# Talking-heads attention with a gated layer: row transfers four partitions higher, loads from SyncE, fp16 pairs in all mixes, rows five units ahead

## The chip, the cores and the metric

The kernel runs on one core of a Trainium2 chip. The metric is the device time of one execution in microseconds. The core's engines are TensorE (PE, with its weight loads shown apart as PEld), VectorE (DVE), ScalarE (ACT), GpSimd (POOL) and SyncE (SP, which only issues DMAs here). Each engine works through its own instructions in order; an instruction that waits holds up all that stand behind it on its engine. PSUM (the banks that TensorE writes to) has eight banks.

## The reference

Four batches, twelve heads, 448 positions, 64 elements per head. The scores of all heads are mixed with each other before the softmax (`w_pre`) and the probabilities after it (`w_post`); the result goes through a gated layer of 1792 tokens, 768 to 1536 to 768.

```python
scores = scale * np.matmul(q, k.transpose(0, 1, 3, 2))
scores = np.einsum('bhij,hg->bgij', scores, w_pre)
scores = scores - np.max(scores, axis=-1, keepdims=True)
attn = np.exp(scores)
attn = attn / (np.sum(attn, axis=-1, keepdims=True) + 1e-09)
attn = np.einsum('bhij,hg->bgij', attn, w_post)
x = np.matmul(attn, v)                       # then (B*S, H*D)
gate = 1.0 / (1.0 + np.exp(-(x @ w_gate)))
out = (gate * (x @ w_val)) @ w_out
```

The weights of the gated layer come as 64-bit floats and are converted on the core.

## The kernel before

**Blocks and units.** Each batch's 448 query rows are cut into blocks of 120, 120, 120 and 88 rows, 16 blocks in all. A block is cut into *units* of two row sets of ten rows each; a batch has 23 units (6 + 6 + 6 + 5; the last holds one set), the kernel 92.

**What is done to a block and a unit.** `scores` multiplies q and k of two heads (six such jobs per block, L149), and `keep` copies them to an SBUF buffer `st`, one head by ACT and one by DVE (L155). There are two `st` buffers, for even and odd blocks. To mix heads on TensorE, the heads of a row must lie across partitions: `regroup` (L179 to L185) does this with DMAs from `st` to a tile `T`, one per half x: 120 partitions for a unit of two sets (five rows of twelve heads each, twice), and, for such a unit, two more DMAs of four partitions (7 KB each) that complete T's second part to 124 partitions. `premix` (L194) multiplies T by the first mix, into one PSUM bank `pm` per set; `rowmax` (L199, DVE) takes the negative maximum; `expo` (L206, ACT) the exponential with its row sum; `norm` (L211 POOL, L212 DVE) one over that sum. `scale` then multiplies by it on POOL, in one of two ways. For units 6 to 83 (`pairs`) it writes an fp16 high half `ph` of the scaled probabilities (L222), `p_lo` (L234, DVE) the fp16 low half `pl`, and `postmix` (L246) is three fp16 products per set, key block and half. For the first 6 and the last 8 units it scales the small second mix matrix instead (`w2s`, L227), and `postmix` is one float32 product with the exponentials themselves. `mix` (L254, ACT) copies the result from the pair of banks `mx` to SBUF. There is one such pair, so the next unit's `postmix` waits for this copy. `av` (L269) multiplies a finished block by v, 16 matmuls per job, and ACT scales the result (L277) and stores it as x in device memory (L278).

**What sets the order.** The loop over slots s issues, in this order: the rows of unit s + LEAD (LEAD = 4; three T buffers); `norm` and `scale` of unit s + 1; `premix` and `rowmax` of unit s + 2; a score job of the next block and its two copies between the exponentials of unit s + 2; `p_lo` of unit s + 1; the loads that are planned for this slot; the gated layer's work that is due; `postmix` of unit s; `mix` of unit s; `av`, and with it the scaling and the store of x. The loads are planned at L291 to L302: v at a batch's slots 4, 6 and 8, k of the next batch in six slots, q four slots ahead of its block's scores.

**Queues.** The rows go from SP's queue. q, k, v, x and the first four raw weight tiles of the gated layer go from ACT's, and so in ACT's own order: each load stands there between the exponentials and the `mix` copy of its slot. The gated layer's x tiles of the first two batches are read back from POOL's queue (L821).

**The gated layer** (`_Moe`) is planned by list scheduling before anything is issued (`order_tasks`). Its matrices are kept as sums of two rounded parts (ACT rounds, L824; DVE takes the rest, L827) and multiplied in seven products per block instead of eight. Raw weights are loaded (L787), converted by ACT and DVE (L795 to L806), written out once and read back. `ROOM` gives the number of buffers of each kind that come free at four times; V is one of the kinds for weight parts. The first of this work runs beside the last units of the attention.

Of the kernel before, what the change touches and what calls it, by code (L numbers as in the profile page):

```python
# [22 lines left out]
R = 10  # L23
# [18 lines left out]
def _attention(ctx, tc, ins, B, H, S, D, xs, raws, make_moe):  # L42
# [18 lines left out]
                          for n, b in (("t", 3), ("e", 3), ("p", 2), ("s", 4)))  # L61
# [64 lines left out]
    def k_load(b, c, eng=None):  # L126
        t = kst.tile([128, S], F32, tag="k", name="k")
        (eng or nc.scalar).dma_start(out=t, in_=kp[b, c])
        k_t[b, c] = t

    def q_load(bi, eng=None):

        b, i0, _, _, sets = blocks[bi]
        n = R * sets
        t = qst.tile([128, NP * QB], F32, tag="q", name="q")
        (eng or nc.scalar).dma_start(out=t[:, :NP * n], in_=qp[b, :, NP * i0:NP * (i0 + n)])
        q_t[bi] = t[:, :NP * n].rearrange("p (c s) -> p c s", s=n)
# [22 lines left out]
    def v_load(b, u):  # L160
        t = vst.tile([128, QUAD, 4, D], F32, tag="v", name="v")
        nc.scalar.dma_start(out=t.rearrange("p h j d -> p (h j d)"), in_=vb[b, u])
# [3 lines left out]
    t_t, nm_t, e_t, ss_t, p_t, mx_t = {}, {}, {}, {}, {}, {}  # L166
    mixes = [mp.tile([128, 4, H, QB], F32, name=f"mix{i}") for i in range(2)]

    def pairs(u):

        return PB + 2 <= u < NU - 8

    def regroup(u):
        bi, r0s, _, _, i = units[u]
        sets, st = blocks[bi][4], st_t[bi]
        T = tp.tile([128, 2, S], F32, tag="T", name="T")
        for x in range(2):
            if len(r0s) == 2:
                nc.sync.dma_start(out=T[:2 * HK, x], in_=st[i + x:sets * R:sets])  # L179
            else:  # L180
                nc.sync.dma_start(out=T[:HK, x], in_=st[i + sets * HALF * x:sets * HALF * (x + 1):sets])
        if len(r0s) == 2:
            p = i + sets * HALF
            for x in range(2):
                nc.sync.dma_start(out=T[2 * HK:64 + HK, x], in_=st[p + x:p + x + 1, :64 - HK])  # L185
        t_t[u] = T

    def premix(u):
        T = t_t.pop(u)
        banks = units[u][2]  # L190
        for x in range(2):
            for i, bank in enumerate(banks):
                rows = slice(64 * i, 64 * i + HK)
# [20 lines left out]
    def scale(u):  # L214

        p_t[u] = []
        for i in range(len(units[u][1])):
            e, ss = e_t[u][:, i], ss_t[u][:, i:i + 1]
            if pairs(u):
                if i == 0:  # L220
                    ph = pp.tile([128, 2, S], F16, tag="ph", name="ph")
                nc.gpsimd.tensor_scalar(ph[:, i], e, ss, 1.0, op0=ALU.mult, op1=ALU.mult)  # L222
                p_t[u].append(ph[:, i])
            else:
                if i == 0:
                    w = pp.tile([128, 2, HK], F32, tag="ph", name="w2s")
                nc.gpsimd.tensor_scalar(w[:, i], w2, ss, 1.0, op0=ALU.mult, op1=ALU.mult)  # L227
                p_t[u].append((e, w[:, i]))

    def p_lo(u):  # L230
        if pairs(u):
            pl = pp.tile([128, 2, S], F16, tag="pl", name="pl")
            for i, ph in enumerate(p_t[u]):
                nc.vector.scalar_tensor_tensor(pl[:, i], e_t[u][:, i], ss_t[u][:, i:i + 1], ph,  # L234
                                               op0=ALU.mult, op1=ALU.subtract)
                p_t[u][i] = (ph, pl[:, i])

    def postmix(u):
        mx = two_banks(ps_mx, "mx").rearrange("p x (i c) -> p x i c", i=2)[:, :, :, :4 * HK]
        for i, (a, b) in enumerate(p_t.pop(u)):  # L240
            terms = [(a, w2hi), (a, w2lo), (b, w2hi)] if pairs(u) else [(a, b)]
            for jb in range(4):
                for k, (lhs, w) in enumerate(terms):
                    for x in range(2):
                        rows = slice(64 * x, 64 * x + 64)
                        nc.tensor.matmul(mx[:, x, i, jb * HK:(jb + 1) * HK], lhsT=lhs[rows, JB[jb]:JB[jb] + 128], rhs=w[rows],  # L246
                                         start=(k == 0), stop=(k == len(terms) - 1))
# [12 lines left out]
    def av(bi, c):  # L260
# [10 lines left out]
        if c % 4 == 3 or c == KC - 1:  # L271
# [6 lines left out]
            nc.scalar.dma_start(out=xs[b, c0:c + 1, :, i0:i0 + n].rearrange("c p s -> p c s"), in_=xt)  # L278


    LEAD = 4
# [51 lines left out]
    q_load(1)  # L333
# [643 lines left out]
```

## Time and profile before

| | |
|---|---|
| median of 3 runs | 876.36 us (872.37 to 903.53) |
| profiled execution | 877.92 us, span 876.1 us, mean granted TensorE clock 0.971 |
| PE busy | 830.4 us, 95% |
| DVE busy | 658.4 us, 75% |
| ACT busy | 557.8 us, 64% |
| POOL busy | 138.5 us, 16% |
| DMA | 136.74 MB, mean 156 GB/s |

The span is the time from the first to the last instruction on the core. A busy PE is not PE at its peak. The granted clock is a share of 2.4 GHz; its lower level is half, 1.2 GHz. Shares are means over stages with different limits: attention to about 396 us, then the gated layer. Where a row ends in square brackets, it tells how long the engine sat idle before that instruction and what released it; releasers are inferred from semaphore events.

### The profile page before, as it was taken

Reading aid. Unit: us, or ns where it says so; the run is one execution under the profiler, and the core shown is the slowest. Engines: PE = TensorE matmul, PEld = TensorE weight load, DVE = VectorE, ACT = ScalarE, POOL = GpSimd, SP = SyncE. Lnnn points to the kernel's source line nnn. Section 1 sums busy time; section 2 is a strip of 40 time slices with the busy share of each in tenths; the row PEclk is TensorE's granted clock in tenths of the full one; section 3 lists DMA queues with packets and bytes.
Section 4 is the critical chain, followed back from the end, with each engine's and each line's share of the span. In section 5 each row is a group of like instructions: output and inputs, shape, how many; then the busy total and the mean of one; then the engine's idle time right before and its main releaser. Section 6 shows DMA issues by size and latency. Waiting matters only on the chain.

```text
span 876.1 us, 22591 instructions
## 1 busy us (share of the span) xinstructions
PE 830.4 (95%) x9314; PEld 647.7 (74%) x9314; DVE 658.4 (75%) x1003; ACT 557.8 (64%) x967; POOL 138.5 (16%) x284
## 2 busy tenths in 40 slices
PE   8989988999899978899999999959999999999998
PEld 2555555565556545689899999949999999999997
DVE  4487887888788866259888788999786676579970
ACT  3678786888788777566776679845544444454640
POOL 0143443434344435210000000000000000000000
PEclk9999999999999999669999999979999999999999
DMA  5375457545754565721655668875251222200001
GB/s 169 143 238 184 158 168 240 183 160 180 248 169 162 185 233 198 268 71 39 241 210 181 208 216 288 296 272 202 82 182 55 66 64 63 73 19 1 32 31 64
DMA packets 70335, 136.74 MB, mean 156 GB/s; under 512 B 19000, under 2 KB 50648, under 8 KB 70232
## 3 DMA queue, kind: packets, MB, share of 16 engines
q1 hardware_dynamic: 49176, 108.17, 35.4%
q10 hardware_dynamic: 20288, 24.37, 9.2%
q0 software_dynamic: 768, 2.75, 1.1%
q8 instruction: 73, 1.20, 0.6%
q14 instruction: 30, 0.25, 0.1%
HBM read 70.14 MB, written 25.17 MB: 109 GB/s over the span
## 4 chain that ended last, share of the span: by engine, by line
PE 80%; DMA 7%; ACT 5%; DVE 4%; SPq 2%; issue 1%; ACTq 1%; DVEq 0%
PE bank L837 35%; PE bank L848 15%; PE mx L246 8%; PE av L269 8%; PE pm L194 8%; PE qk L149 5%; DMA T<-st 5%; ACT mix L254 2%; DMA raws<-in_w_dram 2%; SPq L179 1%; ACT e L206 1%; DVE m_GV L827 1%; DVE m_FWTR L830 1%; DMA k<-in_kp_dram 1%; ACT st L155 1%
## 5 line engine op out<-in xcount | busy, mean ns | idle before, releaser
L837 PE MATMUL bank<-m_GV 128*128 128x448 f32 x1512 | 310.6, 367 | 1.3 <-DVE m_GV L827 0.7
L837 PEld LDWEIGHTS bank<-m_GV 128*128 128x128 f32 x1512 | 284.1, 188 | 27.3 <-DVE m_GV L827 1.1
L827 DVE TENSOR_TENSOR m_GV<-m_FWTR,m_GV 128x768 fp32r<-128x768 f32 (+1 forms) x139 | 156.0, 1135 | 53.6 <-ACT m_GV L824 53.3
L824 ACT CAST m_GV<-m_FWTR 128x768 fp32r<-128x768 f32 (+1 forms) x139 | 134.3, 980 | 62.3 <-DVE m_FWTR L830 24.2
L848 PE MATMUL bank<-m_GV 128*128 128x448 f32 x756 | 161.0, 375 | 9.3 <-ACT m_GV L824 8.2
L848 PEld LDWEIGHTS bank<-m_GV 128*128 128x128 f32 x756 | 145.4, 193 | 24.6 <-ACT m_GV L824 8.9
L206 ACT ACTIVATE e<-pm,nm 128x448 f32<-128x448 f32 x180 | 114.8, 638 | 59.1 <-DVE nm L199 50.5
L199 DVE TENSOR_REDUCE nm<-pm 128x1 f32<-128x448 f32 x180 | 104.0, 619 | 52.3 <-PE pm L194 50.8
L254 ACT ACTIVATE mix<-mx 128x960 f32<-128x960 f32 (+1 forms) x92 | 102.6, 1116 | 31.7 <-PE qk L149 9.6
L246 PEld LDWEIGHTS <-ph 64*128 64x128 f16 x2448 | 56.3, 93 | 72.7 <-issue 40.2
L854 ACT COPY m_FWTR<-bank 128x448 f32<-128x448 f32 x96 | 51.2, 533 | 80.7 <-PE bank L837 57.7
L222 POOL TENSOR_SCALAR ph<-e,ss 128x448 f16<-128x448 f32 x153 | 96.2, 642 | 33.1 <-DVE ss L212 24.0
L194 PE MATMUL pm<-T,w 60*64 60x448 f32 x720 | 96.9, 576 | 1.9 <-DMA T<-st 1.8
L269 PE MATMUL av<-mix,v 128*64 128x120 f32 (+1 forms) x1504 | 97.3, 276 | 0.0
L234 DVE SCALAR_TENSOR_TENSOR pl<-e,ss,ph 128x448 f16<-128x448 f32 x153 | 97.3, 676 | 0.0
L149 PE MATMUL qk<-k,q 64*64 64x448 f32 (+2 forms) x640 | 94.0, 548 | 2.5 <-ACT st L155 2.1
L269 PEld LDWEIGHTS av<-mix,v 128*64 128x64 f32 x1504 | 77.6, 143 | 6.8 <-issue 2.4
L857 DVE TENSOR_TENSOR m_FWTR<-bank,m_FWTR 128x448 f32<-128x448 f32 x90 | 55.9, 622 | 35.5 <-PE bank L848 21.0
L246 PE MATMUL mx<-w2hi,ph 64*128 64x60 f16 x1224 | 60.1, 188 | 20.8 <-ACT mix L254 20.7
L830 DVE TENSOR_TENSOR m_FWTR<-m_FWTR 128x768 f32<-128x768 f32 (+1 forms) x67 | 77.4, 1167 | 0.1
L149 PEld LDWEIGHTS qk<-k,q 64*64 64x64 f32 (+2 forms) x640 | 27.1, 135 | 50.2 <-issue 30.0
L246 PE MATMUL mx<-w2hi,pl 64*128 64x60 f16 x1224 | 59.7, 187 | 0.0
(58 smaller groups left out, 687.0 us busy)
## 6 DMA issues: line engine op xcount, KB each, us to landing
T<-st SPq DMA_DIRECT2D x176, 210.0 KB
raws<-in_w_dram SPq DMA_DIRECT2D x32, 767.6 KB
w<-m_FWTR SPq DMA_DIRECT2D x36, 384.0 KB
m_FWTR<-w SPq DMA_DIRECT2D x30, 384.0 KB
raws<-w SPq DMA_DIRECT2D x18, 384.0 KB
v<-in_vb_dram ACTq DMA_DIRECT2D x12, 512.0 KB
out_dram<-m_FWTR SPq DMA_DIRECT2D x24, 224.0 KB
k<-in_kp_dram ACTq DMA_DIRECT2D x18, 224.0 KB
```

The source lines that it names most:

```text
L149: nc.tensor.matmul(sc[e][s0:s1, :S], lhsT=q[rows, c, s0:s1], rhs=k[rows, :], start=True, stop=True)
L194: nc.tensor.matmul(pm[bank][64 * x:64 * x + 64, :S], lhsT=w1[rows], rhs=T[rows, x], start=True, stop=True)
L199: nc.vector.tensor_reduce(nm[:, i:i + 1], pm[bank][:, :S], axis=AX.X, op=ALU.max, negate=True)
L206: nc.scalar.activation(out=e_t[u][:, i], in_=pm[units[u][2][i]][:, :S], func=AF.Exp, bias=nm_t[u][:, i:i + 1], scale=1.0, accum_out=ss_t[u ...
L234: nc.vector.scalar_tensor_tensor(pl[:, i], e_t[u][:, i], ss_t[u][:, i:i + 1], ph, op0=ALU.mult, op1=ALU.subtract)
L246: nc.tensor.matmul(mx[:, x, i, jb * HK:(jb + 1) * HK], lhsT=lhs[rows, JB[jb]:JB[jb] + 128], rhs=w[rows], start=(k == 0), stop=(k == len(te ...
L254: nc.scalar.activation(out=out.rearrange("p g (y r) -> p y g r", r=HALF), in_=mx_t.pop(u), func=AF.Copy, scale=1.0 / (P_UP * W_UP))
L269: nc.tensor.matmul(av_t[bi][64 * i:64 * i + 64, c % 4, :n], lhsT=vt[b, u][:, h + i, jb, :], rhs=mixes[bi % 2][:, jb, 2 * c + i, :n], start ...
L824: self.nc.scalar.copy(self.f32(hi).bitcast(F32R), self.f32(f))
L827: self.nc.vector.tensor_tensor(self.f32(lo).bitcast(F32R), self.f32(f), self.f32(hi), op=ALU.subtract)
L837: self.nc.tensor.matmul(self.f32(bank), lhsT=w[a][:, k], rhs=x[b][:, k], start=self.START[i] and k == r == 0, stop=k == self.KH - 1 and r ...
L848: self.nc.tensor.matmul(self.f32(bank), lhsT=w[a][:, k], rhs=b[bb], start=self.START[i] and j == k == r == 0, stop=j == OUT_TILES - 1 and ...
```

## The change

It makes seven edits. T's rows lie at partitions 4 to 123 instead of 0 to 119: the first set at 4 to 63, the second at 64 to 123. The first mix's matmul for the first set now reads partitions 0 to 63, of which the first four are zero in T (set once by POOL) and in the matrix, so the two four-partition transfers fall away. There are four T buffers, used in turn. Every unit uses fp16 pairs. All loads and the stores of x are issued by SP, but for the three small mix matrices and the second block's q tile, which stay with ACT. LEAD is 5. In `ROOM`, V has one buffer less from 15 slots before the layer and one more at its start. Beside this the names move: `t_t` and `pairs` are gone.

```diff
-                          for n, b in (("t", 3), ("e", 3), ("p", 2), ("s", 4)))
+                          for n, b in (("t", 1), ("e", 3), ("p", 2), ("s", 4)))
...
     def k_load(b, c, eng=None):
...
-        (eng or nc.scalar).dma_start(out=t, in_=kp[b, c])
+        (eng or nc.sync).dma_start(out=t, in_=kp[b, c])
...
     def q_load(bi, eng=None):
...
-        (eng or nc.scalar).dma_start(out=t[:, :NP * n], in_=qp[b, :, NP * i0:NP * (i0 + n)])
+        (eng or nc.sync).dma_start(out=t[:, :NP * n], in_=qp[b, :, NP * i0:NP * (i0 + n)])
...
     def v_load(b, u):
...
-        nc.scalar.dma_start(out=t.rearrange("p h j d -> p (h j d)"), in_=vb[b, u])
+        nc.sync.dma_start(out=t.rearrange("p h j d -> p (h j d)"), in_=vb[b, u])
...
-    t_t, nm_t, e_t, ss_t, p_t, mx_t = {}, {}, {}, {}, {}, {}
+    nm_t, e_t, ss_t, p_t, mx_t = {}, {}, {}, {}, {}
...
-    def pairs(u):
-        return PB + 2 <= u < NU - 8
+    t_bufs = [tp.tile([128, 2, S], F32, name=f"T{i}") for i in range(4)]
+    for T in t_bufs:
+        nc.gpsimd.memset(T[:64 - HK], 0.0)
     def regroup(u):
...
-        sets, st = blocks[bi][4], st_t[bi]
-        T = tp.tile([128, 2, S], F32, tag="T", name="T")
+        sets, st, T = blocks[bi][4], st_t[bi], t_bufs[u % len(t_bufs)]
+        at = 64 - HK
...
-                nc.sync.dma_start(out=T[:2 * HK, x], in_=st[i + x:sets * R:sets])
+                nc.sync.dma_start(out=T[at:at + 2 * HK, x], in_=st[i + x:sets * R:sets])
...
-                nc.sync.dma_start(out=T[:HK, x], in_=st[i + sets * HALF * x:sets * HALF * (x + 1):sets])
-        if len(r0s) == 2:
-            p = i + sets * HALF
-            for x in range(2):
-                nc.sync.dma_start(out=T[2 * HK:64 + HK, x], in_=st[p + x:p + x + 1, :64 - HK])
-        t_t[u] = T
+                nc.sync.dma_start(out=T[at:at + HK, x], in_=st[i + sets * HALF * x:sets * HALF * (x + 1):sets])
     def premix(u):
-        T = t_t.pop(u)
+        T = t_bufs[u % len(t_bufs)]
...
-                rows = slice(64 * i, 64 * i + HK)
+                rows = slice(64, 64 + HK) if i else slice(0, 64)
...
     def scale(u):
-        p_t[u] = []
+        ph = pp.tile([128, 2, S], F16, tag="ph", name="ph")
...
-            e, ss = e_t[u][:, i], ss_t[u][:, i:i + 1]
-            if pairs(u):
-                if i == 0:
-                    ph = pp.tile([128, 2, S], F16, tag="ph", name="ph")
-                nc.gpsimd.tensor_scalar(ph[:, i], e, ss, 1.0, op0=ALU.mult, op1=ALU.mult)
-                p_t[u].append(ph[:, i])
-            else:
-                if i == 0:
-                    w = pp.tile([128, 2, HK], F32, tag="ph", name="w2s")
-                nc.gpsimd.tensor_scalar(w[:, i], w2, ss, 1.0, op0=ALU.mult, op1=ALU.mult)
-                p_t[u].append((e, w[:, i]))
+            nc.gpsimd.tensor_scalar(ph[:, i], e_t[u][:, i], ss_t[u][:, i:i + 1], 1.0, op0=ALU.mult, op1=ALU.mult)
+        p_t[u] = [ph]
     def p_lo(u):
-        if pairs(u):
-            pl = pp.tile([128, 2, S], F16, tag="pl", name="pl")
-            for i, ph in enumerate(p_t[u]):
-                nc.vector.scalar_tensor_tensor(pl[:, i], e_t[u][:, i], ss_t[u][:, i:i + 1], ph,
-                                               op0=ALU.mult, op1=ALU.subtract)
-                p_t[u][i] = (ph, pl[:, i])
+        pl = pp.tile([128, 2, S], F16, tag="pl", name="pl")
+        for i in range(len(units[u][1])):
+            nc.vector.scalar_tensor_tensor(pl[:, i], e_t[u][:, i], ss_t[u][:, i:i + 1], p_t[u][0][:, i],
+                                           op0=ALU.mult, op1=ALU.subtract)
+        p_t[u].append(pl)
     def postmix(u):
         mx = two_banks(ps_mx, "mx").rearrange("p x (i c) -> p x i c", i=2)[:, :, :, :4 * HK]
-        for i, (a, b) in enumerate(p_t.pop(u)):
-            terms = [(a, w2hi), (a, w2lo), (b, w2hi)] if pairs(u) else [(a, b)]
+        ph, pl = p_t.pop(u)
+        for i in range(len(units[u][1])):
...
-                for k, (lhs, w) in enumerate(terms):
+                for k, (p, w) in enumerate(((ph, w2hi), (ph, w2lo), (pl, w2hi))):
...
-                        nc.tensor.matmul(mx[:, x, i, jb * HK:(jb + 1) * HK], lhsT=lhs[rows, JB[jb]:JB[jb] + 128], rhs=w[rows],
-                                         start=(k == 0), stop=(k == len(terms) - 1))
+                        nc.tensor.matmul(mx[:, x, i, jb * HK:(jb + 1) * HK], lhsT=p[rows, i, JB[jb]:JB[jb] + 128], rhs=w[rows],
+                                         start=(k == 0), stop=(k == 2))
...
-            nc.scalar.dma_start(out=xs[b, c0:c + 1, :, i0:i0 + n].rearrange("c p s -> p c s"), in_=xt)
-    LEAD = 4
+            nc.sync.dma_start(out=xs[b, c0:c + 1, :, i0:i0 + n].rearrange("c p s -> p c s"), in_=xt)
+    LEAD = 5
...
-    q_load(1)
+    q_load(1, nc.scalar)
...
-    ROOM = ((-15, dict(F=5, G=4, W=6, V=4)), (-7, dict(G=2, V=2, T=3)), (0, dict(G=3, W=2, V=2)), (9.6, dict(F=4, G=5, W=2, V=0, T=4, R=0)))
+    ROOM = ((-15, dict(F=5, G=4, W=6, V=3)), (-7, dict(G=2, V=2, T=3)), (0, dict(G=3, W=2, V=3)), (9.6, dict(F=4, G=5, W=2, V=0, T=4, R=0)))
...
     def load_raw(self, k):
-        self.loads.dma_start(out=self.at["raw", k].bitcast(I8)[:, :8 * self.WE - 3], in_=self.src[k].bitcast(I8)[:, 3:])
+        self.nc.sync.dma_start(out=self.at["raw", k].bitcast(I8)[:, :8 * self.WE - 3], in_=self.src[k].bitcast(I8)[:, 3:])
     def top(self, k, step):
...
-            (self.nc.gpsimd if p == 0 else self.nc.sync).dma_start(out=out[:, :, e], in_=src.rearrange("c p s -> p c s"))
+            self.nc.sync.dma_start(out=out[:, :, e], in_=src.rearrange("c p s -> p c s"))
...
     def slot(self, t):
...
-        self.loads = self.nc.scalar if a < -7 else self.nc.sync
...
-            w1[(60 * x + r * H + np.arange(H) - 64) % 60 + 64 if x else at, r * H:(r + 1) * H] = w_pre
+            w1[at.start + 4 * (1 - x):at.stop + 4 * (1 - x), r * H:(r + 1) * H] = w_pre
...

```

**Order on ACT, slots 6 and 7 of the first batch.** The names are the exponential (L206, e), the score copy (L155, st), the loads and the copy of the mix (L254). The brackets hold what an instruction waits for; DMAHW0 to DMAHW7 are semaphores that DMAs of both queues share in turn. Before:

```order
L206 ACTIVATE e,ss<-pm_114,nm 128x448 [waits DVE_49]
L162 DMA v<-in_vb_dram 128x1024 [waits DMAHW6_49]
L128 DMA k<-in_kp_dram 128x448 [waits DMAHW7_49]
L254 ACTIVATE mix_125<-mx 128x4x48x5 [waits PE_49]
L206 ACTIVATE e,ss<-pm_112,nm 128x448 [waits DVE_49,Activation_49,Pool_49]
L155 COPY st<-qk 120x448 [waits PE_49]
L206 ACTIVATE e,ss<-pm_113,nm 128x448 [waits DVE_49]
L128 DMA k<-in_kp_dram 128x448 [waits DMAHW1_49]
L254 ACTIVATE mix_125<-mx 128x4x48x5 [waits PE_49]
```

Now, in the same place (the first copy of a new block waits for the row transfers that read this buffer):

```order
L201 ACTIVATE e,ss<-pm_114,nm 128x448 [waits DVE_49]
L239 ACTIVATE mix_125<-mx 128x4x48x5 [waits PE_49]
L201 ACTIVATE e,ss<-pm_112,nm 128x448 [waits DVE_49,Activation_49,Pool_49]
L155 COPY st<-qk 90x448 [waits DMAHW4_49,DMAHW3_49,DMAHW5_49,DMAHW2_49,DMAHW6_49,DMAHW1_49,DMAHW7_49,DMAHW0_49,PE_49]
L201 ACTIVATE e,ss<-pm_113,nm 128x448 [waits DVE_49]
L239 ACTIVATE mix_125<-mx 128x4x48x5 [waits PE_49]
```

The loads between the exponentials and the mix copy are gone from ACT.

**Order on SP, in the second batch, around the last unit of a block.** A number after st tells the block whose buffer is read, one after T the buffer. Before:

```order
L185 DMA T_2594<-st_1820 4x1x448 x2
L179 DMA T_2687<-st_1820 120x1x448 x2
L185 DMA T_2687<-st_1820 4x1x448 x2
L179 DMA T_2782<-st_1820 120x1x448 x2
L185 DMA T_2782<-st_1820 4x1x448 x2
L179 DMA T_2874<-st_2341 120x1x448 x2
```

Now:

```order
L179 DMA T3_129<-st_1882 120x1x448 x2
L136 DMA q_2575<-in_qp_dram 128x540
L263 DMA xs_60<-xt_2635 128x4x88
L179 DMA T0_126<-st_1882 120x1x448 x2
L162 DMA v_2667<-in_vb_dram 128x1024
L179 DMA T1_127<-st_1882 120x1x448 x2
L128 DMA k_2757<-in_kp_dram 128x448
L263 DMA xs_60<-xt_2817 128x2x88
L179 DMA T2_128<-st_1882 120x1x448 x2
L162 DMA v_2849<-in_vb_dram 128x1024
L128 DMA k_2851<-in_kp_dram 128x448
L179 DMA T3_129<-st_2394 120x1x448 x2
```

The four-partition transfers are gone, and loads and stores of x stand between the rows; the block's last rows (T2_128) come right behind a store of x.

**Order on DVE, two of the last units.** Named are the maxima (nm), one over the sum (ss), the converted raw weights (m_FWTR<-raws) and the low halves (pl). Before:

```order
L212 RECIPROCAL ss<-ss 128x2
L199 TENSOR_REDUCE nm<-pm_114 128x1
L199 TENSOR_REDUCE nm<-pm_112 128x1
L212 RECIPROCAL ss<-ss 128x2
L199 TENSOR_REDUCE nm<-pm_113 128x1
L199 TENSOR_REDUCE nm<-pm_114 128x1
L806 SCALAR_TENSOR_TENSOR m_FWTR<-raws 128x768 x2
```

Now:

```order
L219 SCALAR_TENSOR_TENSOR pl<-e,ss,ph 128x448 x2
L791 SCALAR_TENSOR_TENSOR m_FWTR<-raws 128x768 x2
L207 RECIPROCAL ss<-ss 128x2
L194 TENSOR_REDUCE nm<-pm_112 128x1
L194 TENSOR_REDUCE nm<-pm_113 128x1
L219 SCALAR_TENSOR_TENSOR pl<-e,ss,ph 128x448 x2
L791 SCALAR_TENSOR_TENSOR m_FWTR<-raws 128x768
L207 RECIPROCAL ss<-ss 128x2
```

Two low halves are added per unit; the layer's own instructions keep their sequence, here and on PE and ACT.

## Rows read from the trace of the kernel before

**Rows 1.** Stretches of the run: start:end and length, busy time and count per engine.

```profile
45.00:341.00 296.00, 273.55 (x6165) 162.73 (x6164) 235.77 (x471) 233.31 (x503) 118.93 (x234) 0.99 0.57 191
341.00:381.00 40.00, 35.00 (x376) 27.75 (x370) 19.68 (x29) 22.21 (x39) 13.51 (x27) 0.71 0.64 213
381.00:396.00 15.00, 15.00 (x173) 13.42 (x172) 5.26 (x6) 8.63 (x12) 0.00 (x0) 0.75 0.27 92
...
396.00:876.00 480.00, 465.88 (x2249) 425.00 (x2247) 377.82 (x455) 270.05 (x366) 0.00 (x0) 0.99 0.39 131
```

Engines in the order PE, PEld, DVE, ACT, POOL; then the granted clock, the busy share of the DMA engines and GB/s.

**Rows 2.** Chain of waits over one unit: start, us, what.

```profile
83.00 0.91 PE pm L194 x8
83.91 0.75 PE qk L149 x8
84.66 0.77 PE mx L246 x48
85.43 0.97 PE av L269 x16
```

**Rows 3.** PE's waits, 45 to 341 us: total, times, longest.

```profile
PE mx L246 <- ACT mix L254: 20.7, 18, 2.8
```

**Rows 4.** ACT in order of time, 147 to 151 us: start, us, instruction, idle before.

```profile
149.84 0.33 ACTq L128 DMA_DIRECT2D k<-in_kp_dram  x1
150.23 1.13 ACT L254 ACTIVATE mix<-mx 128x960 f32<-128x960 f32 x1 [2.69 <-DMA T<-st]
```

**Rows 5.** PE in order of time at 320 us.

```profile
320.06 0.20 PE L246 MATMUL mx<-w2hi,ph 64*128 64x60 f16 x2 [1.49 <-ACT mix L254]
```

**Rows 6.** Two stretches, an undisturbed one and one with loads, as in Rows 1.

```profile
82.00:99.00 17.00, 17.00 (x372) 10.25 (x368) 13.40 (x28) 13.58 (x28) 7.28 (x15) 1.00 0.47 152
...
144.00:156.00 12.00, 9.70 (x214) 5.33 (x212) 8.06 (x17) 8.06 (x18) 4.61 (x9) 1.00 0.77 241
```

**Rows 7.** Row transfers, time to issue one on SP: least/median/most ns.

```profile
L179 SPq DMA_DIRECT2D T<-st x176: 788/813/1532, 12.2 to 347.0; - x176
L185 SPq DMA_DIRECT2D T<-st x176: 606/644/1272, 14.0 to 352.2; - x176
```

**Rows 8.** Chain of waits at 311 us.

```profile
311.19 1.79 PE av L269 x16
```

**Rows 9.** ACT in order of time, 103 to 108 us.

```profile
104.57 0.66 ACT L277 ACTIVATE xt<-av,sw 128x480 f32<-128x480 f32 x1
...
106.60 0.52 ACT L155 COPY st<-qk 120x448 f32<-120x448 f32 x1
```

**Rows 10.** The first row transfer and its first user, in order of time.

```profile
12.15 1.83 SPq L179 DMA_DIRECT2D T<-st  x2
...
15.09 2.10 PE L194 MATMUL pm<-T,w 60*64 60x448 f32 x7
```

**Rows 11.** Chain of waits: two landings of row transfers.

```profile
144.62 5.20 DMA T<-st
...
343.00 8.01 DMA T<-st
```

**Rows 12.** Chain of waits in the first units.

```profile
30.78 1.93 PE mx L246 x32
...
34.37 1.93 PE mx L246 x32
```

**Rows 13.** The second mix alone (L246), 341 to 381 us: PE and PEld.

```profile
341.00:381.00 40.00, 18.91 (x220) 18.02 (x222) 0.71 0.64 213
```

**Rows 14.** PE in order of time at 352 us.

```profile
352.69 3.67 PE L246 MATMUL mx<-w2s,e 64*128 64x60 f32 x32 [3.52 <-ACT mix L254]
```

**Rows 15.** ACT in order of time at 351 us.

```profile
351.03 0.35 ACTq L787 DMA_DIRECT2D raws<-in_w_dram  x1
```

**Rows 16.** Groups of instructions by line: count, busy us, mean ns, idle before.

```profile
L234 DVE SCALAR_TENSOR_TENSOR pl<-e,ss,ph 128x448 f16<-128x448 f32 x153 | 97.3, 676 | 0.0
```

## The prediction, made before the changed kernel ran

> **What bounds the kernel now.** I read the stretches of the whole run first. In [rows 1] the reader should see two halves: attention up to 396 us, and the gated layer, 480 us in which PE is busy 465.9. The change leaves the order of the layer's work on PE, DVE and ACT as it was, so I look for its effect before 396. There PE is the bound wherever nothing disturbs it: the chain of waits over one unit is PE alone, 0.91 + 0.75 + 0.77 + 0.97 = 3.40 us [rows 2]. In 45 to 341 us PE is idle for 296.0 - 273.6 = 22.4 us [rows 1]. Nearly all of it, 20.7 us in 18 waits, is the fp16 mix of one unit waiting for ACT to empty the bank pair of the unit before [rows 3].
>
> Why ACT is late then stands in ACT's own order of time [rows 4]: before that copy it issues a load of k, and this issue came only after 2.69 us of idling that ended with the landing of a row transfer of *another* queue. The order rows for ACT say why: the issue waits for a DMA semaphore (DMAHW1) that the rows' transfers use too. I went through the 18 waits one by one: 15 stand behind an issue of v, k, q, a raw weight tile or x on ACT, the other 3 behind ACT's work on raw weights (the longest 1.49 us [rows 5], 3.3 together). Undisturbed and disturbed stretches differ as this asks: PE 17.00 of 17 us, against 9.70 of 12 where loads run [rows 6].
>
> **The change, part by part.**
>
> *Fewer row transfers on SP.* Each pair unit drops two 7 KB transfers of 0.644 us issue, 176 in all, and keeps two of 0.813 us [rows 7]; SP's 2.9 us of issuing per unit falls to 1.6. SP isn't on the chain of [rows 2], so this alone is worth nothing while units take 3.40 us; it pays for the loads that SP takes over (0.33 to 0.4 us each).
>
> *Loads leave ACT.* ACT no longer waits at all in front of the 15 late copies: 20.7 - 3.3 = 17.4 us. One stall also halved PE's clock for a while: the value product after it took 1.79 us [rows 8] instead of 0.97 [rows 2], at 1.2 instead of 2.4 GHz after PE had idled; with its neighbours about 2 us. Gain 19.4 us. Against it stands a new wait. On SP the rows of a block's last unit now queue behind a store of x, which waits for ACT's scaling (order rows for SP); and the first score copy two slots later overwrites the buffer that these rows are read from. I work out whether they land in time. The scaling ends at 104.57 + 0.66 = 105.23; the next slot's score copy starts at 106.60, the one after it a unit later at 110.00 [rows 9]: 4.8 us. The path needs 0.4 us for the store's issue, 1.66 for two row issues, and the landing: in an empty stretch about 2.1 us (first issue ends near 13.0 us, PE starts on it at 15.09) [rows 10], in a loaded one 5.20 [rows 11]. So 4.2 us fits, and 7.3 us is 2.5 late. There are 14 such block ends; loads of k and v run at one in four of them, so I take 3 late ones, 7 us. Ends: 0 and 14 x 2.5 = 35. I take **13 us** (19.4 - 7, rounded).
>
> The Trainium skill (DMA: Bandwidth & Descriptors, "Issuing engines are not separate DMA queues") says that issuing from several engines only saves the issuing sequencer's time, which is usually small. By it the loads' move is worth about 15 issues of 0.4 us, 6 us instead of 17.4. [Rows 4] speak against it: the issue took 0.33 us and the wait ahead of it 2.69.
>
> *Rows five units ahead, four buffers.* The rows get a slot more, 3.40 us, before PE needs them, so that SP's later issue is hidden; without that slot a loaded landing would reach PE. The start has one more score job before the first mix and one fewer after it; the rows come sooner because the small transfers are gone. I take 0, ends -2 and +2 (one issue group of 1.3 us, a little more for a job).
>
> *fp16 pairs in the first 6 units.* PE's mix falls from 1.93 to 0.77 us, the unit from 3.60 (30.78 to 34.37) [rows 12] to 0.91 + 0.75 + 0.77 = 2.43. But POOL now scales whole rows, and DVE makes the low half: with these, five units cost DVE 13.40 and ACT 13.58 us [rows 6], 2.7 each. So a unit ends between 2.7 and 3.4; I take 3.1, nearest to the units without a value product. 6 x 0.5 = **3 us**, ends 1 and 5.
>
> *fp16 pairs in the last 8 units, the x loads and raw loads on SP.* From 341 to 381 us PE is busy 35.0 of 40 [rows 1], 18.9 of it float32 mixes [rows 13], 7 of them. The stretch holds the longest stall, 3.52 us, and after it PE at half clock: a mix takes 3.67 us [rows 14]. ACT stood behind a raw load's issue until 351.03 us [rows 15]; that goes. With 7 x 0.77 = 5.4 us of mixes PE needs 21.5. DVE gets 13 low halves of 0.676 us [rows 16]: 19.7 + 8.8 = 28.5; ACT keeps 22.2. So DVE is the bound, at 28.5 if it were never kept waiting, against 40 now: up to 11.5; I take 8, since DVE and ACT pass the rounding of the weights to and fro. From 381 to 396 PE is busy throughout at a clock of 0.75 [rows 1]; at full clock 15 becomes 11.2: 4. Together **12 us**, ends 5 and 16. If the clock stays at half, PE's 21.5 are still under DVE's 28.5, and only the 4 are lost.
>
> *One V buffer less before the layer, one more at its start.* The order of work is unchanged: 0, ends -4 and +4. PE idles 480.0 - 465.9 = 14.1 us in the layer [rows 1]; nothing here touches that.
>
> Sum: 13 + 0 + 3 + 12 + 0 = 28 us. The profiled execution took 877.92 us; 877.9 - 28 = 850, and as it lies 1.6 above the median of the runs, 876.36, I predict **848 us**.
>
> **Rivals.**
> 1. *The new wait eats what the loads' move gives.* If loaded landings are met at 6 or 8 of the 14 block ends, 15 to 20 us go: 848 + 13 = 861. For it: SP passes through more waits than before, all in order. Against: loads run in 4 to 11 of a batch's 23 units only. A chance of 0.14.
> 2. *Only the issue time counts.* PE gains 6 instead of 17.4 us as SP, too, is held up by the same semaphores: 848 + 11 = 859. A chance of 0.08.
> 3. *Slower: the rows stand behind the loads on one queue.* Loads and rows were on two queues; now each k, v or raw tile is ahead of the rows that are issued after it. If the landing grows as in the most crowded stretch, 8.01 us [rows 11], the path is 10.1 us, 5.3 late, at all 14 ends: 74 - 7 = 67 us more, 848 + 67 = 915. It decides from a mean lateness of (28 + 7) / 14 = 2.5 us, a landing of 5.2 us everywhere, where the gain is gone; beyond 3.7 us the kernel is slower by over 2%. Against: that crowd is the x loads' alone, and 10 of 14 ends lie in empty stretches. A chance of 0.06. On this bears the Trainium skill (DMA: Bandwidth & Descriptors, "Queues, rings and completion order"): SP and ACT own one row of rings each, and an engine goes round the rows packet by packet, so that rows on a ring of their own get turns that they lose behind loads on the same ring. No row here shows the two on one ring.
> 4. *The layer takes it back.* If the layer started earlier than its weights are ready, it would stall; then 870. DVE is busy in 377.8 of its 480 us [rows 1], yet most of its order there begins only where the attention ends. A chance of 0.04.
>
> **How the numbers follow.** My forecast has 0.68. About 2%, 17.5 us, is what a measurement of this kernel can tell from no change: 858.9 or less is faster. Good ends (19, 16, 5, 2 and 4 us, less than all at once) lead to some 832; rivals 1 and 2 reach to 863, half of 859 to 863 outside the faster case. I take 830 to 866. Faster: 0.68 and a third of rivals 1 and 2, 0.75. Within 2%: the rest of these and rival 4, 0.19. Slower: 0.06.
>
> **What would show it.** In the profile after: no DMA issue on ACT after the first microseconds; PE's wait for ACT's mix copy under 8 us in the stretch up to the last 8 units, and no more waits of ACT on a landing of rows ahead of it. First units under 3.3 us apart, with fp16 mixes of 0.77. No 3.5 us stall before the last units, the clock above 0.9 in the tail, and the layer's first matmuls some 28 us sooner, with the layer as long as before. A new ACT or DVE wait on row transfers in front of a score copy at each block's end would make rivals 1 or 3 right; PE waiting for rows in front of the first mix would say that SP's queue is the new bound.

## The result, and the profile after

The changed kernel takes **842.5 us** (median of 4 runs, 841.9 to 843.2); the kernel before took 875.5 beside it. The ratio is 0.963, 95% interval 0.9605 to 0.9663. Its profiled execution took 842.77 us, with a span of 841.0 (before: 877.92 and 876.1).

Stretches of the changed kernel, in the columns of [rows 1]:

```profile
45.00:306.00 261.00, 251.30 (x5676) 148.03 (x5678) 217.91 (x432) 213.21 (x460) 116.13 (x215) 0.99 0.59 191
...
306.00:346.00 40.00, 32.21 (x770) 21.19 (x766) 33.17 (x60) 32.07 (x65) 16.79 (x30) 0.96 0.81 262
346.00:362.00 16.00, 14.90 (x268) 13.30 (x261) 12.83 (x15) 12.66 (x19) 0.83 (x2) 0.79 0.47 154
362.00:841.00 479.00, 464.96 (x2250) 424.46 (x2249) 378.55 (x456) 270.67 (x367) 0.00 (x0) 0.99 0.39 132
```

In the middle of the attention PE is now busy 96.3% of the time (251.30 of 261), against 92.4% (273.55 of 296) [rows 1]. The tail before the layer is shorter, and the layer starts near 362 instead of 396 and lasts as long as before (479 us).

The changed kernel's DMA queues (queue, packets, MB, share of 16 engines); q1 is SP's, q10 is ACT's:

```profile
q1 hardware_dynamic: 70680, 133.53, 47.8%
...
q10 hardware_dynamic: 576, 0.51, 0.2%
```

Its waits of PE in units 5 to 83, 41 to 322 us (total, times, longest), which answer to [rows 3]:

```profile
PE mx L231 <- ACT mix L239: 5.5, 7, 2.0
PE qk L149 <- ACT st L155: 3.4, 4, 1.2
```

And of ACT's score copies (st) on landings, in the same stretch:

```profile
ACT st L155 <- DMA k<-in_kp_dram: 2.6, 1, 2.6
...
ACT st L155 <- DMA T<-st: 0.3, 1, 0.3
```

The row of 2.6 us bears a load's name, but it is the new wait that the prediction feared, as e10 bears out, where it is gone. The copy is the first of a new block, and the rows that it must wait for were issued right behind a store of x. SP, then ACT, in order of time:

```profile
205.37 0.38 SPq L263 DMA_DIRECT2D xs<-xt  x1
205.85 1.69 SPq L179 DMA_DIRECT2D T<-st  x2
...
212.18 0.53 ACT L155 COPY st<-qk 90x448 f32<-90x448 f32 x1 [2.56 <-DMA k<-in_kp_dram]
```

Loads have left ACT, PE's wait for the mix copy has fallen from 20.7 us [rows 3] to 5.5, about a quarter, and the new wait is small: 2.9 us on ACT. So far everything looks as foretold. The experiments show that this reading gives the gain to the wrong edit.

For the comparison by stages I take from ACT's order of time when the mix copies of units 0, 5, 83 and 91 (the last) start. In the changed kernel the first of them are:

```profile
25.90 1.13 ACT L239 ACTIVATE mix<-mx 128x960 f32<-128x960 f32 x1
29.01 1.13 ACT L239 ACTIVATE mix<-mx 128x960 f32<-128x960 f32 x1
32.03 1.14 ACT L239 ACTIVATE mix<-mx 128x960 f32<-128x960 f32 x1
```

All runs, in us; the stages and the span are of each run's profiled execution, the ratio is to the kernel before on the same chip. The medians come from several chips, on which the kernel before took 875.5 to 882.2, so a difference of a few us between medians is better read from the ratios:

| run | median | ratio, 95% interval | to unit 0 | 0 to 5 | 5 to 83 | 83 to 91 | rest | span |
|---|---|---|---|---|---|---|---|---|
| before | 875.5 | 1 | 29.2 | 18.1 | 292.7 | 45.5 | 490.6 | 876.1 |
| changed | 842.5 | 0.963 (0.9605-0.9663) | 25.9 | 15.2 | 281.1 | 31.0 | 487.9 | 841.0 |
| e1 loads back | 842.5 | 0.959 (0.9550-0.9634) | 26.0 | 15.2 | 276.3 | 33.2 | 487.6 | 838.2 |
| e2 loads alone | 894.0 | 1.018 (1.0138-1.0227) | 29.5 | 18.0 | 308.8 | 41.7 | 496.4 | 894.4 |
| e3 float32 early | 848.3 | 0.967 (0.9628-0.9713) | 26.0 | 18.0 | 283.1 | 28.3 | 488.5 | 843.9 |
| e4 float32 late | 852.5 | 0.970 (0.9659-0.9742) | 26.1 | 15.2 | 280.2 | 31.6 | 491.6 | 844.6 |
| e5 small alone | 854.0 | 0.969 (0.9609-0.9762) | 25.7 | 18.0 | 276.6 | 41.7 | 489.2 | 851.1 |
| e6 small back | 883.5 | 1.005 (1.0012-1.0095) | 27.7 | 21.3 | 308.7 | 33.7 | 489.8 | 881.2 |
| e7 small, loads back | 872.8 | 0.995 (0.9900-0.9996) | 27.3 | 21.0 | 299.4 | 33.0 | 489.8 | 870.4 |
| e8 lead 4 | 850.9 | 0.969 (0.9609-0.9773) | 25.2 | 15.2 | 287.5 | 30.7 | 488.3 | 846.9 |
| e9 split | 845.9 | 0.960 (0.9578-0.9622) | 25.5 | 15.2 | 277.5 | 32.5 | 492.0 | 842.6 |
| e10 x store later | 841.6 | 0.955 (0.9529-0.9570) | 25.9 | 15.2 | 276.6 | 29.4 | 490.9 | 837.9 |
| e11 changed again | 844.3 | 0.960 (0.9560-0.9635) | 26.1 | 15.2 | 280.6 | 29.4 | 488.5 | 839.7 |
| e12 small and fp16 | 840.8 | 0.956 (0.9515-0.9598) | 25.3 | 15.2 | 274.4 | 33.5 | 487.8 | 836.2 |

### The profile page after: what moved, and what is told of

Read it like the earlier page. It is cut to its first block, busy times and chain, and to the rows that moved or that the text cites. A ratio compares the mean times of both kernels' runs of the same rounds, so it can differ in the third digit from the quotient of the medians.

```text
span 841.0 us, 22853 instructions
## 1 busy us (share of the span) xinstructions
PE 802.4 (95%) x9530; PEld 625.0 (74%) x9530; DVE 674.6 (80%) x1030; ACT 557.5 (66%) x967; POOL 150.1 (18%) x280
## 4 chain that ended last, share of the span: by engine, by line
PE 84%; ACT 6%; DMA 4%; DVE 3%; issue 1%; SPq 1%; POOL 0%; ACTq 0%; DVEq 0%
PE bank L822 37%; PE bank L833 18%; PE av L254 9%; PE pm L189 7%; PE qk L149 7%; PE mx L231 6%; ACT e L201 2%; ACT mix L239 1%; DMA T<-st 1%; DMA k<-in_kp_dram 1%; ACT st L155 1%; DVE nm L194 1%; DMA raws<-in_w_dram 1%; DMA raws<-w 1%; DMA m_FWTR<-w 0%
## 5 line engine op out<-in xcount | busy, mean ns | idle before, releaser
L822 PEld LDWEIGHTS bank<-m_GV 128*128 128x128 f32 x1512 | 283.5, 188 | 27.3 <-DVE m_GV L812 1.1
L809 ACT CAST m_GV<-m_FWTR 128x768 fp32r<-128x768 f32 (+1 forms) x139 | 134.2, 980 | 62.2 <-DVE m_FWTR L815 24.8
L194 DVE TENSOR_REDUCE nm<-pm 128x1 f32<-128x448 f32 x180 | 103.8, 617 | 32.1 <-PE pm L189 30.7
L231 PEld LDWEIGHTS <-ph 64*128 64x128 f16 x2880 | 66.8, 94 | 75.3 <-issue 37.7
L213 POOL TENSOR_SCALAR ph<-e,ss 128x448 f16<-128x448 f32 x180 | 112.6, 638 | 43.0 <-DVE ss L207 28.0
L219 DVE SCALAR_TENSOR_TENSOR pl<-e,ss,ph 128x448 f16<-128x448 f32 x180 | 115.9, 684 | 1.2 <-POOL ph L213 1.2
L254 PE MATMUL av<-mix,v 128*64 128x120 f32 (+1 forms) x1504 | 95.3, 271 | 1.6 <-issue 1.6
L189 PE MATMUL pm<-T,w 64*64 64x448 f32 (+1 forms) x720 | 95.7, 568 | 0.7 <-ACT e L201 0.7
L231 PE MATMUL mx<-w2hi,ph 64*128 64x60 f16 x1440 | 71.2, 189 | 15.1 <-ACT mix L239 13.9
L254 PEld LDWEIGHTS av<-mix,v 128*64 128x64 f32 x1504 | 75.5, 140 | 6.9 <-issue 2.6
L231 PE MATMUL mx<-w2lo,ph 64*128 64x60 f16 x1440 | 70.7, 188 | 0.5 <-issue 0.5
L231 PE MATMUL mx<-w2hi,pl 64*128 64x60 f16 x1440 | 70.7, 188 | 0.0
```

The lines of the kernel that those rows point to most:

```text
L189: nc.tensor.matmul(pm[bank][64 * x:64 * x + 64, :S], lhsT=w1[rows], rhs=T[rows, x], start=True, stop=True)
L194: nc.vector.tensor_reduce(nm[:, i:i + 1], pm[bank][:, :S], axis=AX.X, op=ALU.max, negate=True)
L213: nc.gpsimd.tensor_scalar(ph[:, i], e_t[u][:, i], ss_t[u][:, i:i + 1], 1.0, op0=ALU.mult, op1=ALU.mult)
L231: nc.tensor.matmul(mx[:, x, i, jb * HK:(jb + 1) * HK], lhsT=p[rows, i, JB[jb]:JB[jb] + 128], rhs=w[rows], start=(k == 0), stop=(k == 2))
L254: nc.tensor.matmul(av_t[bi][64 * i:64 * i + 64, c % 4, :n], lhsT=vt[b, u][:, h + i, jb, :], rhs=mixes[bi % 2][:, jb, 2 * c + i, :n], start ...
L809: self.nc.scalar.copy(self.f32(hi).bitcast(F32R), self.f32(f))
```

## The experiments

Theory A is the prediction's: ACT's issues made PE wait, so moving the loads pays. The rival is that SP's queue, with four row transfers per unit, was what ACT's issues waited for, so dropping two of them pays wherever the loads stand (theory B in the first texts, C in the later ones).

**e1: the loads' move undone in the changed kernel.** The edit for k; q, v, x stores, raw weights and x loads go back likewise to where they were.

```diff
-        (eng or nc.sync).dma_start(out=t, in_=kp[b, c])
+        (eng or nc.scalar).dma_start(out=t, in_=kp[b, c])
...
```

> The changed kernel (842.5 us) with every load and store that the change took from ACT (and the first x loads from POOL) issued there again; all else as changed. Theory A (ACT's issues are what made PE wait): the 17 us of waits for ACT's mix copies come back in part, 13 us up to the last 8 units, and the stall before the last units with its slow clock costs up to 8 more: 855 to 863 us. Theory B (SP's dropped small transfers already freed the shared semaphores, so ACT's issues would not wait any more): under 5 us, 842 to 847, and PE's wait for the mix copy stays under 10 us.

842.5 us, and a ratio of 0.959 against 0.963: nothing is lost, as the rival said. PE's waits in units 5 to 83, 41.2 to 317.5 us:

```profile
PE mx L231 <- ACT mix L239: 7.2, 10, 3.2
PE qk L149 <- ACT st L155: 1.4, 3, 0.5
```

With the loads on ACT the mix waits are 7.2 us here, near the changed kernel's 5.5 and far from the 20.7 of [rows 3]. Theory A falls.

**e2: the loads' move alone, in the kernel before.** The edit for k; all other loads and the x stores likewise.

```diff
-        (eng or nc.scalar).dma_start(out=t, in_=kp[b, c])
+        (eng or nc.sync).dma_start(out=t, in_=kp[b, c])
...
```

> The kernel before (876) with only the loads moved: k, q, v, x and raw weights are issued from SP; small transfers, float32 mixes and four slots of lead stay. Theory A (the move by itself is what pays): 13 to 20 us sooner, 856 to 863. Rival (SP with 2.9 us of row issues per unit of 3.4 has no room for the loads, so the rows come late and PE waits ahead of its first mix): 870 to 890, and the trace shows PE or ACT waiting for row transfers.

894.0 us, 1.8% slower than before and beyond the rival's own figure. PE's waits in units 5 to 83, 47.5 to 356.3 us, and ACT's on rows:

```profile
PE pm L194 <- DMA T<-st: 10.6, 8, 3.1
PE mx L246 <- ACT mix L254: 4.3, 6, 1.0
```

```profile
ACT st L155 <- DMA T<-st: 11.0, 7, 5.3
```

The mix wait is nearly gone (4.3 of 20.7 us), as theory A says it must be; but rows come late, and PE stands ahead of its first mix instead. These waits of PE do not add up to the 16.1 us that the stage grew by, because a part of the lateness lies inside PE's busy time. The first mix in units 5 to 83, the kernel before and then e2 (busy us, mean ns, idle before):

```profile
L194 PE MATMUL pm<-T,w 60*64 60x448 f32 x612 | 77.1, 563 | 0.0
...
L194 PE MATMUL pm<-T,w 60*64 60x448 f32 x612 | 94.8, 571 | 10.6 <-DMA T<-st 10.6
```

The same 612 matmuls keep PE busy 17.7 us longer, though one of them takes nearly as long as before (571 against 563 ns), so they overlap less; the weight loads ahead of them (PEld) wait for the rows, again before and in e2:

```profile
PEld pm L194 <- DMA T<-st: 1.4, 9, 0.2
...
PEld pm L194 <- DMA T<-st: 17.5, 20, 3.3
```

A stall removed on ACT comes back on SP.

**e5: the small transfers dropped alone, in the kernel before.**

```diff
-                nc.sync.dma_start(out=T[:2 * HK, x], in_=st[i + x:sets * R:sets])
+                nc.sync.dma_start(out=T[at:at + 2 * HK, x], in_=st[i + x:sets * R:sets])
...
-        if len(r0s) == 2:
-            p = i + sets * HALF
-            for x in range(2):
-                nc.sync.dma_start(out=T[2 * HK:64 + HK, x], in_=st[p + x:p + x + 1, :64 - HK])
...
```

> The kernel before (876) with only the rows landing four partitions higher, so that the two small transfers per pair unit fall away; loads stay on ACT, four slots of lead, three row buffers, float32 mixes in the first and last units. The theory of the prediction (SP's issues are off the path, this is worth 0): 872 to 878. New theory C (eight DMA semaphores are handed round to all transfers; with four row transfers per unit a load on ACT waits for the semaphore of a row transfer of two units before, with two of four units before): the waits of ACT's loads go, 10 us up to the last 8 units, some 8 in the tail and 1 to 3 at the start: 850 to 862, and PE's wait for ACT's mix copy falls from 20.7 us to under 8.

854.0 us, inside theory C's range: this edit, which the prediction put at 0, is the largest of all. First the kernel before, SP in order of time around the stall of [rows 4]:

```profile
142.90 1.68 SPq L179 DMA_DIRECT2D T<-st  x2
144.62 1.93 SPq L185 DMA_DIRECT2D T<-st  x2
146.66 1.68 SPq L179 DMA_DIRECT2D T<-st  x2
148.82 1.45 SPq L185 DMA_DIRECT2D T<-st  x2
150.39 1.68 SPq L179 DMA_DIRECT2D T<-st  x2
```

Two units of rows take from 142.90 to 150.39, 3.75 us each, and SP's issues, with the waits between the two of a pair, fill 6.74 of these 7.49 us: here SP is slower than the 3.40 us of PE's chain [rows 2]. The load on ACT waits until 149.84 for a landing out of this late queue. The landing itself is a large part of the lateness: the chain of waits starts it at 144.62 and gives it 5.20 us [rows 11], and 144.62 is when a pair of the 7 KB transfers (L185) is issued. Two more of the late loads follow the same pattern; in the chain of the kernel before, each of these landings starts with a 7 KB pair:

```profile
58.54 5.25 DMA T<-st
...
63.81 0.33 ACTq L128
...
229.04 5.05 DMA T<-st
...
234.12 0.33 ACTq L128
```

So these loads wait for the very transfers that the edit leaves out. The same load as at 149.84, in e5, ACT in order of time:

```profile
136.66 0.33 ACTq L128 DMA_DIRECT2D k<-in_kp_dram  x1
...
137.86 1.12 ACT L253 ACTIVATE mix<-mx 128x960 f32<-128x960 f32 x1
```

No idle time stands in front of the copy, where 2.69 us stood before. What SP waited for, 45 to 341 us, shows its slack; the kernel before, its three largest rows (all ten sum to 85.9 us):

```profile
SPq L179 <- DVE st L155: 24.4, 14, 3.3
SPq L179 <- PE qk L149: 23.1, 26, 2.5
SPq L179 <- ACT e L206: 15.5, 14, 3.3
```

and e5 (all fourteen sum to 240.0 of 296 us):

```profile
SPq L183 <- PE qk L149: 83.5, 45, 3.8
SPq L183 <- DVE st L155: 45.8, 14, 3.8
SPq L183 <- PE pm L193: 32.0, 26, 3.4
```

In e5 SP stands ready most of the time, and two thirds of that time ends with PE, whose first mix frees the row buffers. Before, it also waited about once a unit, but 1 us or so each time: slack on average, with little to spare where a unit is disturbed.

**e6 and e7: the small transfers back in the changed kernel, with the loads on SP (e6) and on ACT (e7).** The edit is e5's, reversed; e7 adds e1's.

> The changed kernel (842.5) with the two small transfers per pair unit back and the rows four partitions lower; loads on SP, five slots of lead, four buffers, fp16 mixes as changed. Prediction's theory: 0 lost, 842 to 846. Theory C: SP issues 2.9 us of rows and the loads in units of 3.4 us, rows come late as in the run of the loads alone, PE waits for them ahead of its first mix: 860 to 885.

> The changed kernel with both undone: small transfers back, and loads issued from ACT and POOL as before; what stays of the change are the fp16 mixes, five slots of lead and four row buffers. Theory C: ACT's loads wait again for the semaphores of row transfers two units back, 855 to 872. Rival D (the fifth slot and the fourth buffer let the rows go out sooner, so that their semaphores are free in time): 842 to 850.

883.5 and 872.8 us: e6 is inside theory C's range and e7 0.8 us beyond its slow end; rival D falls. In e6, ACT's wait on rows, and PE behind it, 10 to 306 us:

```profile
ACT st L155 <- DMA T<-st: 22.5, 9, 4.8
```

```profile
PE qk L149 <- ACT st L155: 20.5, 9, 5.3
```

In e7 the old stalls, same stretch:

```profile
ACT mix L241 <- DMA T<-st: 11.4, 6, 3.4
```

```profile
PE mx L233 <- ACT mix L241: 20.2, 18, 2.9
```

With the small transfers in, each queue for the loads has its own stall of some 20 us: the wait for the mix copy on ACT, the block's last rows behind the loads and x stores on SP. That second one is the prediction's new wait, at three times its size.

**e8: four slots of lead in the changed kernel.**

```diff
-    LEAD = 5
+    LEAD = 4
```

> The changed kernel with four slots of lead instead of five (four row buffers, all else as changed). Prediction's theory: within 2 us, 840.5 to 844.5. Rival: the fifth slot is what hides the loads in SP's queue; without it PE waits for rows ahead of its first mix, 5 to 10 us more, 847 to 853.

850.9 us, 7 to 8 more than the changed kernel; the ratio's interval is wide (0.9609 to 0.9773) and overlaps the changed kernel's, so the rows have to speak. PE and then ACT, 10 to 306 us:

```profile
PE pm L189 <- DMA T<-st: 4.7, 8, 1.8
```

```profile
ACT st L155 <- DMA T<-st: 7.2, 2, 4.2
```

The changed kernel's list has no such row of PE, and 2.9 us of ACT's with the one under a load's name. With loads on SP the fifth slot is needed; stage 5 to 83 grows from 281.1 (280.6 in e11) to 287.5.

**e12: small transfers dropped and fp16 mixes everywhere; the loads, four slots and three buffers as before.** The edit against e1's kernel:

```diff
-    t_bufs = [tp.tile([128, 2, S], F32, name=f"T{i}") for i in range(4)]
+    t_bufs = [tp.tile([128, 2, S], F32, name=f"T{i}") for i in range(3)]
...
-    LEAD = 5
+    LEAD = 4
```

> Small transfers dropped and fp16 mixes in every unit, but loads on ACT and POOL, four slots of lead and three row buffers as in the kernel before. Theory C (the fifth slot pays only where loads stand in SP's queue ahead of the rows; fp16 mixes are worth 6 to 14 us over the run with small transfers dropped alone, 854): 840 to 848, as the changed kernel. Rival (the fifth slot is worth its 8 us here too): 848 to 854.

840.8 us: two of the change's parts give all of it. (e12 also has the change's room for V, which no run tried alone; the layer took 480 us before and 479 in the changed kernel.) In 45 to 306 us PE is busy 98% of the time:

```profile
45.00:306.00 261.00, 256.01 (x5818) 151.00 (x5816) 222.77 (x444) 218.50 (x471) 113.41 (x221) 1.00 0.62 201
```

**e3 and e4: float32 mixes again in the first units, and in the last 8.** The scaling, the low half and the mix have both branches again; the edit of e3 (e4 returns `u < NU - 8`):

```diff
+    def pairs(u):
+        return u >= PB + 2
...
```

> The changed kernel with float32 mixes again in the first batch's first 7 units (as before the change); all else as changed. Theory A: 0.5 us for each of six units, 3 us later (ends 1 and 5): 843.5 to 847.5; the first mix still ends 2 us or more sooner than in the kernel before, because the start's gain is not the mixes'. Rival: the start's 3.3 us belong to the fp16 pairs as well, and then 6 us are lost: 848.5.

> The changed kernel with float32 mixes again in the last 8 units; all else as changed. Theory A (the fp16 pairs gave most of the tail's 14.5 us): 8 us or more are lost, 850 to 855. Rival (the tail's gain is the raw loads' leaving ACT, which removed the 3.52 us stall and the half clock behind it, and the fp16 pairs only trade PE's time for DVE's): 0 to 4 us are lost, 842 to 847, and the clock in the tail stays above 0.9.

e3's median, 848.3, lies above theory A's range and at the rival's figure; its stages still speak for theory A: units 0 to 5 take 18.0 instead of 15.2 us, 2.8 for five units, and unit 0 comes as early as in the changed kernel, so the start's gain isn't the mixes'. Where its slower executions (up to 853.2) lose more than the profiled one (845.7) isn't shown. For e4 the profile and the median disagree. The profiled execution, 300 to 356 us:

```profile
300.00:356.00 56.00, 48.91 (x874) 36.20 (x874) 35.56 (x62) 47.00 (x87) 15.44 (x37) 1.00 0.73 237
```

At full clock throughout, its tail takes 31.6 us, 0.6 more than the changed kernel's; that run took 846.4 us at a mean clock of 0.992. The other five took 849.9 to 854.8 at 0.979 to 0.988. So with the raw loads on SP, float32 mixes were nearly as fast in one execution of six; where the other five lost their time was not profiled. e5's tail shows the slow way, float32 with the loads on ACT:

```profile
346.00:362.00 16.00, 16.00 (x136) 13.36 (x134) 7.63 (x9) 9.29 (x12) 3.17 (x4) 0.50 0.34 114
```

PE is busy all the time, at 1.2 GHz.

**e9, e10, e11: can the changed kernel be bettered?** e9 issues k, q, v and the x stores from ACT, raw weights and x loads from SP. e10 puts each x store behind the next unit's rows (the loop stands after the call of regroup in the loop over slots):

```diff
-            nc.sync.dma_start(out=xs[b, c0:c + 1, :, i0:i0 + n].rearrange("c p s -> p c s"), in_=xt)
+            later.append((xs[b, c0:c + 1, :, i0:i0 + n].rearrange("c p s -> p c s"), xt))
...
+        while later:
+            o, t = later.pop(0)
+            nc.sync.dma_start(out=o, in_=t)
...
```

> The changed kernel with k, q, v and the x stores issued from ACT again, raw weights and x loads left on SP. Theory C, with the stages of the two kernels it is mixed from (units 5 to 83 in 276.3 us with the loads on ACT against 281.1 on SP; the last 8 units in 31.0 on SP against 33.2 on ACT): 835 to 840 us, 2 to 7 sooner than the changed kernel on the same chip. Rival (the difference between these two was one execution's scatter): 841 to 844, not to be told apart.

> The changed kernel with each x store on SP put behind the rows of the next unit instead of ahead of them; all else as changed. The prediction's term for the new wait (a block's last rows stand behind an x store that waits for ACT, and the next score copy waits for them) was 7 us: if it has that size, 835 to 838. Theory C (with SP's issues at 1.6 us a unit the rows are in time behind the store all the same, the trace has 0.3 us of it): 0 to 2 us, 840 to 843.

> The changed kernel as it is, on the chip of the two runs beside it, to hold them against: 842.5 us (841 to 845).

e9: 845.9 against e11's 844.3, no gain; my sum of two stages was one execution's scatter, as the rival said, though 845.9 is 1.9 us above the rival's own range. e10: 841.6, 2.7 less than e11 beside it: inside theory C's range, and far from 7. Stage 5 to 83 takes 276.6 instead of 280.6 us, the level of the runs with the x stores on ACT (276.3, 277.5): the store ahead of the rows costs about 4 us of that stage, and e10 has neither of the two ACT rows of 2.6 and 0.3 us. The intervals of e10 and of the changed kernel's second measurement overlap, as does that of e12; the first measurement's, 0.9605 to 0.9663 on another chip, lies above both. So no version beats the changed kernel beyond doubt, but e12 needs half of its edits.

## Why the prediction was right, and which of its steps were wrong

842.5 lies 5.5 us below the forecast and well inside the range, on the forecast's side. But the sum came right with its largest terms on the wrong edits, and so by luck. The runs make a path of profiled spans from before to changed, one part at a time (e12 also takes the change's V room):

| part (spans) | predicted gain | measured |
|---|---|---|
| small transfers dropped (876.1 to 851.1) | 0 | 25.0 |
| fp16 mixes at both ends (851.1 to 836.2) | 3, and much of 12 | 14.9 |
| fifth slot, fourth buffer (836.2 to 838.2) | 0 | -2.0 |
| loads to SP (838.2 to 841.0) | 13, and some of 12 | -2.8 |

These are single executions on several chips. Fast runs of the changed kernel on one chip lie up to 10 us apart (e11: 841.5 to 851.9), so the last two steps can't be told from nothing; the first two are borne out by the ratios (1 to 0.969 to 0.956).

*Fewer row transfers: the step that failed.* "SP isn't on the chain of [rows 2], so this alone is worth nothing while units take 3.40 us". [Rows 2] are an undisturbed unit. In the units that PE lost time in, [rows 4] already name the culprit: ACT's issue ended its wait with a landing of *rows*, and [rows 11] start it where a 7 KB pair was issued. I read it by who waited (ACT) and not by who was late (SP's queue), and took away the waiter. Alone, the edit gives 16.1 us in units 5 to 83, where I expected 13 from the loads; 3.5 before unit 0, where I took 0 with an end of 2 (e2, with the small transfers in, has none of it); and 3.8 in the tail.

*Loads leave ACT: wrong.* Its 19.4 us weren't there to be had once the small transfers were gone (e1), and with them in, the move costs 16 (e2). The other half of that sentence, that dropping them "pays for the loads that SP takes over", holds: e6 is some 40 us above the changed kernel. The new wait was found rightly and mis-sized: 3 late block ends and 7 us expected, two late ends (2.6 and 0.3 us) and about 4 us of stage in the kernel as changed (e10), 20.5 with the small transfers (e6).

The Trainium skill (DMA: Bandwidth & Descriptors, "Issuing engines are not separate DMA queues") says that issuing from several engines saves only the issuing sequencer's time, usually small beside the transfer. I let [rows 4] overrule it. Between e1 and the changed kernel the runs agree with it: 842.5 and 842.5. In e2, where SP already issues 2.9 us of rows in units of 3.40 us, the same move costs 16 us; how much of that is issuing time isn't shown.

*Five slots ahead: 0 by luck.* The fifth slot pays for the loads on SP (some 6 us of span in e8) and gives nothing without them.

*fp16 in the first units: right*, 2.8 of 3 by e3's stage.

*The tail: right in size* (45.5 to 31.0, 14.5 against 12), its parts not settled. Between e5 and e12 the fp16 mixes take it from 41.7 to 33.5, about the 8 us that I took for them, with the raw loads still on ACT; the loads' move, which I named for the longest stall, adds 2.2 (e1 against changed). But in e4's profiled execution the move without the fp16 mixes has a tail of 31.6, so the two are not simply added. The clock came back to 0.96, but fell to 0.79 in the last 16 us, after a shorter stall. PE in the changed kernel, and what ACT did before it, in order of time:

```profile
342.50 2.04 ACT L809 CAST m_GV<-m_FWTR 128x768 fp32r<-128x768 f32 x2
344.44 1.13 ACT L239 ACTIVATE mix<-mx 128x960 f32<-128x960 f32 x1
...
345.62 0.20 PE L231 MATMUL mx<-w2hi,ph 64*128 64x60 f16 x2 [2.57 <-ACT mix L239]
```

The mix copy stood behind the rounding of weights (L809) here, not behind a load's issue.

*The layer: right*, 480.0 to 479.0; the edit of V's room was not run alone.

The rivals: rival 2 (only issue time counts) had the right view of the loads' move and the wrong sum, since it gave the small transfers nothing either. Rivals 1 and 3 are what e6 and e2 became: the rows behind the loads, 0.5% and 1.8% slower than before. What kept them away is the edit that I priced at 0.

What I named as signs (no issues on ACT, the mix wait under 8 us, first units under 3.3 apart, the layer 28 us sooner) nearly all came true; the clock did not, at 0.79 in the last 16 us, and ACT still waited 2.9 us on rows. e12 would show all but the first as well (its mix wait is 6.4 us from 10 to 315 us). They could confirm the sum, but not the cause.

*Left open.* Dropping two of four transfers does three things. It gives SP back 1.3 us per unit. It moves the last user of a load's DMA semaphore further back, by count (loads left out) from two units to four, since the order rows show eight of them (DMAHW0 to 7) handed round. And it takes away the 7 KB transfers whose landings, 5.05 to 5.25 us after their issue, the late loads stood waiting for. Which of these ends the waits wasn't told apart: every transfer left out or added changes all three.

## What to carry to other kernels

When an instruction waits for a landing, ask first why that transfer was late, and follow its queue back, before moving the instruction that waits; an undisturbed unit doesn't show what the disturbed ones are bound by. Count a queue's issues per unit against the unit's time: at 2.9 of 3.4 us it had slack on average and hardly any in the disturbed units. And when a change has several parts that would leave the same signs in a profile, undo one at a time: here about half of the edits gave all of the gain, and of the others the fifth slot only paid for the loads' move.

## What the runs showed of the hardware

A transfer of 7 KB costs the engine that issues it nearly as much as one of 210 KB: 0.644 against 0.813 us of issuing [rows 7]. And it can land late: in the three loaded stretches above, 5.05 to 5.25 us after its issue. With the small ones gone, the issue of the large one also became a little shorter; the changed kernel's row transfers (least/median/most ns):

```profile
L179 SPq DMA_DIRECT2D T<-st x176: 768/775/2128, 12.2 to 329.7; - x176
```

SP waited for others in 85.9 of 296 us, so it was 71% used at most, and yet loads that take 0.33 to 0.4 us each to issue made the whole kernel 1.8% slower when they were put there (e2).
